# Windowed attention into a squared-ReLU expert layer on one core: the weights' words are joined in a PSUM bank, their low parts go to GpSimd, 15 squares go to VectorE, and the order of work is laid out again

## The chip, the core and the metric

One core of a Trainium2 chip runs the whole program as one launch. The metric is the device time in microseconds; lower is better. The engines are named as the profile names them: PE (TensorE matmul), PEld (its weight loads), DVE (VectorE), ACT (ScalarE), POOL (GpSimd) and SP (SyncE, which issues the DMAs).

## What is computed

The reference, cut to what matters (batch 4, 8 heads, 768 positions, head size 64; 3072 tokens, model width 512, hidden width 2048; all fp32):

```python
for c in range(nc):                     # chunks of 32 queries
    k_full = concat([mem_k, k[:, :, l_start:r_end]])   # 8 memory keys, 16 left, 8 right
    v_full = concat([mem_v, v[:, :, l_start:r_end]])
    a = softmax(scale * q_c @ k_full.T)
    out[:, :, c_start:c_end] = a @ v_full
x = attention output as [3072 tokens, 512]
h = x @ w_in
g = s * maximum(h, 0) ** 2 + b
y = g @ w_out
```

The two weight matrices reach the chip as 64-bit floating point words, seen as pairs of 32-bit integers. The kernel itself turns each into a high fp32r part and a low fp32r part, and every product of the expert layer is made of three matmuls (low x high, high x low, high x high).

## The kernel before, in words

**Tokens and stages.** The tokens fall into five groups: three plain groups of 384 tokens (`ch` 0, 1, 2) and two groups of 960 tokens that are done later by a scheme of seven products on 2x2 blocks (`seven`, `rest`). Attention is done in 40 visits (`attend`): scores on PE, mask and maximum on DVE (`L533`), exponential on ACT (`L537`), a reciprocal and a multiplication by it on POOL (`L546`, `L549`), a transposition on PE (`L558`) or on DVE (`L569`), the product with the values on PE (`L498`).

**Steps.** The plain groups are done in 48 steps (`STEPS`). A step takes one slice `f` of 128 hidden units for one token group: 12 matmuls for h (`hidden`, `L611`), then on ACT relu, square, affine and a high copy in place in a PSUM bank (`L619` to `L622`, the last into `gH`), on DVE the low part `gL` (`L623`), and 9 matmuls into the result (`result`, `L636`). The first 8 steps are group 0 with slices 0 to 7, the next 16 are group 1 with slices 0 to 15, then group 0 with slices 8 to 15, then group 2. So a weight slice that is needed for the first time is met by steps 0 to 7 and 16 to 23. A step is counted from 0; its `gH` is called the first one for step 0.

**Weights.** `weight(i, half, f, due)` turns one of 32 tiles of 128x512 into its two parts. ACT scales the high words into a buffer `wv` (`L586`); DVE shifts the low words (`L587`), joins them with the buffer (`L589`) and puts the sign in (`L591`); ACT copies the result to the high part of `w` (`L595`); DVE subtracts to get the low part (`L596`). One tile thus costs ACT two instructions and DVE four. There are five buffers `wv` and four buffers `words`. Ten tiles come through the `early` buffers. After all tiles are there, `blocks` makes sums of weight blocks for the seven products on POOL (`L694`, `L702`), splits them on ACT and DVE (`L705`, `L706`) and sends them to DRAM.

**The order.** Nothing of the order is written out by hand. Each operation is given an engine, a hold time from the table `HOLD`, a priority (mostly the step at which it is due) and a `lock` flag; `Plan.lay` runs a list scheduler over them at build time, gives out buffers and PSUM banks from rings, and the instructions are then emitted in that order. Operations with the flag on DVE and on POOL are not laid over each other. While a PSUM bank is spare, in the first 40 us of the plan, PE is given filler matmuls (`warm`, `L371`) where it has nothing else. Eight PSUM banks are shared by scores, values, h, result accumulators and products (`room`).

Of the kernel before, what the change touches and what calls it, by code (L numbers as in the profile page):

```python
# [11 lines left out]
F32 = mybir.dt.float32  # L12
F32R = mybir.dt.float32r
I32 = mybir.dt.int32
# [32 lines left out]
LATE_SUMS = 3  # L47
AHEAD = 8.0
# [47 lines left out]
HOP = 2500.0  # L96
WIRE, ALONE = 365.0, 200.0
SLOW, NSLOW, NFIRST = 290.0, 10, 20
FLIGHT = 8
BIG, NEAR = 600, 1500.0  # L100
# [63 lines left out]
class Plan:  # L164
# [25 lines left out]
    def lay(self, filler=None):  # L190
# [18 lines left out]
        while todo:  # L209
# [6 lines left out]
            for e in engines:  # L216
# [37 lines left out]
                if got is None:  # L254
                    if e == "PE" and filler and filler[0](t):
                        laid.append((t, -1, None))
                        free[e] = t + HOLD["warm"]
                        heapq.heappush(events, free[e])
                    continue
# [39 lines left out]
def body(ctx: ExitStack, tc: tile.TileContext, qkv, w1, w2, out):  # L299
# [49 lines left out]
    def room(r, kind):  # L349
        n = r.live.get  # L350
        if kind == "acc":
            r.free += spare
            spare.clear()
            return n("acc", 0) < NT
        if kind == "p":
            return n("p", 0) < 5
# [53 lines left out]
    def anchor(n):  # L410

        ch, c = divmod(n, H // 2)
        if ch == 0:
            return -30 + 2 * c
        if ch < NALONE:
            return starts[ch] - LEAD - 2.0 * (H // 2 - 1 - c)
        i = n - NALONE * (H // 2)
        k = min(i, (NPLAIN - NALONE) * (H // 2) + PB + DEPTH)
        return VISITS[0] + VISITS[1] * k + VISITS[2] * (i - k)
# [156 lines left out]
    def weight(i, half, f, due):  # L576
        src = (w1, w2)[half][f]
        raw = Early(i, 0, 2 * DM) if i < NEARLY - 6 else Val(words)
        v, w = Val(wvs), c_w[half, f]
        both = lambda: raw.tile.bitcast(I32).rearrange("p (n two) -> p n two", two=2)  # L580
        lo, hi = (lambda: both()[:, :, 0]), (lambda: both()[:, :, 1])
        bits = lambda: v.tile.bitcast(I32)
# [3 lines left out]
        op("ACT", "wscale", due, lambda: nc.scalar.activation(v.tile, hi().bitcast(F32), AF.Copy, scale=2.0 ** -112), (raw["hi"],), (v[0],))  # L586
# [3 lines left out]
           (raw["lo"],), (v[0],), lock=True)  # L590
        op("DVE", "wsign", due, lambda: nc.vector.scalar_tensor_tensor(bits(), hi(), -2147483648, bits(), ALU.bitwise_and, ALU.bitwise_or),  # L591
           (raw["hi"],), (v[0],), lock=True)
# [3 lines left out]
        op("DVE", "wjoin", due, lambda: nc.vector.tensor_tensor(  # L596
# [7 lines left out]
    def hidden(u):  # L604
# [13 lines left out]
        ahead = AHEAD if u >= NSLACK else 1.0  # L618
        op("ACT", "relu", u - ahead, lambda: nc.scalar.activation(hp(), hp(), AF.Relu), (), (h[0],))  # L619
        op("ACT", "square", u - ahead, lambda: nc.scalar.activation(hp(), hp(), AF.Square), (), (h[0],))  # L620
# [66 lines left out]
    def blocks(side, g, due):  # L687

        fs = (2 * g, 2 * g + 1)
        parts = [[c_w[side, f]["H"], c_w[side, f]["L"]] for f in fs]  # L690
        sums, high = (Val(words) for _ in range(2))
# [63 lines left out]
    def mix(p):  # L755

        due = base(p) - 6.0
# [230 lines left out]
    for i, (due, half, f) in enumerate(ORDER):  # L988
        weight(i, half, f, due - 1.5)
# [74 lines left out]
```

## Time and profile before, and how to read it

| | us |
|---|---|
| median of 3 runs (595.2 to 597.22) | 595.73 |
| the profiled execution | 596.2 |
| its span, first to last instruction | 594.4 |
| PE busy | 584.0 (98%) |
| PEld busy | 493.7 (83%) |
| DVE busy | 453.1 (76%) |
| ACT busy | 427.2 (72%) |
| POOL busy | 186.2 (31%) |

Busy times are unions over the span; the ends of matmuls are modelled, so a PE that reads 95% busy can still be waiting for operands, and the pace of its matmuls has to be read from their starts. An instruction's own duration is longer than the distance to the next instruction's start on the same engine, since neighbours overlap; costs below are distances between starts where there are rows for them. The averages hide that the engines are loaded differently in different stretches: DVE and ACT are full in the first 100 us and have room later.

### The profile page before, as it was taken

The numbers are of one execution on the slowest core, as the hardware profiler recorded it, in microseconds if no ns is written. First come the engines' busy times: TensorE is split into PE (matmuls) and PEld (weight loads), VectorE is DVE, ScalarE is ACT, GpSimd is POOL, SyncE is SP. The second block draws the span as 40 slices with busy tenths as digits, with TensorE's granted clock in tenths as the row PEclk, the third lists the DMA queues.
The fourth block names the chain that finished last, engine by engine and source line by source line (L and its number), as shares of the span: only waits on it lengthen the run. The fifth ranks groups of instructions, "written<-read, shape, count | busy, mean of one in ns | idle before, by whom it ended". The sixth has DMA issues, their size and how long they took to land.

```text
span 594.4 us, 10771 instructions
## 1 busy us (share of the span) xinstructions
PE 584.0 (98%) x3483; PEld 493.7 (83%) x3487; DVE 453.1 (76%) x1231; ACT 427.2 (72%) x1093; POOL 186.2 (31%) x202
## 2 busy tenths in 40 slices
PE   9999999999999999999999999999999999999997
PEld 4787788888888788888888888888888888888886
DVE  5799999955878877889999777999643443399654
ACT  6999999776878789878787876667533645555552
POOL 4522210187777775713773322000000111000000
PEclk9999999999999999999999999999999999999999
DMA  8953656134899999995789667577766555666761
GB/s 290 406 204 101 224 186 214 63 118 143 277 332 323 358 354 346 320 380 179 259 318 391 244 222 278 194 234 226 241 230 233 207 202 192 207 195 199 241 212 66
DMA packets 71383, 142.78 MB, mean 240 GB/s; under 512 B 7072, under 2 KB 43808, under 8 KB 71328
## 3 DMA queue, kind: packets, MB, share of 16 engines
q1 hardware_dynamic: 71184, 141.99, 70.2%
q8 instruction: 27, 0.44, 0.3%
q14 instruction: 28, 0.23, 0.1%
q10 hardware_dynamic: 144, 0.12, 0.1%
HBM read 102.50 MB, written 39.58 MB: 239 GB/s over the span
## 4 chain that ended last, share of the span: by engine, by line
PE 76%; DVE 10%; ACT 6%; POOL 2%; DMA 2%; issue 2%; SPq 1%; DVEq 0%; POOLq 0%; ACTq 0%
PE ps L824 25%; PE ps L946 25%; PE ps L636 10%; PE ps L611 9%; PE ps L461 4%; PE ps L498 3%; ACT t L537 2%; DVE w L596 2%; DVE t L533 2%; DVE wv L591 2%; DVE wv L589 1%; POOL words L702 1%; ACT wv L586 1%; PE ps L371 1%; DVE words L587 1%
## 5 line engine op out<-in xcount | busy, mean ns | idle before, releaser
L824 PE MATMUL ps<-again,again 128*128 128x480 f32 x672 | 149.0, 381 | 0.0
L824 PEld LDWEIGHTS ps<-again,again 128*128 128x128 f32 x672 | 125.6, 188 | 20.9
L611 PE MATMUL ps<-x,w 128*128 128x384 f32 x576 | 112.3, 340 | 0.3 <-DVE w L596 0.3
L537 ACT ACTIVATE t<-t,nmax 96x128 f32<-96x128 f32 x256 | 99.7, 393 | 13.7 <-DVE nmax L533 13.6
L611 PEld LDWEIGHTS ps<-x,w 128*128 128x128 f32 x576 | 100.4, 188 | 6.6 <-DVE w L596 0.5
L636 PE MATMUL ps<-w,gH 128*128 128x512 f32 x288 | 90.3, 395 | 0.5 <-DVE w L596 0.5
L946 PE MATMUL ps<-gH,again 128*128 128x482 f32 x272 | 81.5, 380 | 0.0
L569 DVE STREAM_TRANSPOSE aT<-t 32x256 f32<-32x256 f32 x168 | 73.0, 435 | 5.4 <-POOL t L549 2.5
L549 POOL TENSOR_TENSOR t<-t,rden 96x1024 f32<-96x1024 f32 (+1 forms) x40 | 61.9, 1552 | 35.1 <-DVE words L587 10.5
L533 DVE CUSTOM_DVE_ANT_0 t<-ps,mask 96x128 f32<-96x128 f32 x256 | 58.5, 281 | 18.2 <-PE ps L461 17.9
L636 PEld LDWEIGHTS ps<-w,gH 128*128 128x128 f32 x288 | 54.0, 188 | 11.2 <-DVE w L596 0.8
L946 PE MATMUL ps<-again,again 128*128 128x482 f32 x264 | 62.0, 382 | 0.0
L636 PE MATMUL ps<-w,gL 128*128 128x512 f32 x144 | 58.2, 404 | 3.8 <-DVE gL L623 3.8
L946 PEld LDWEIGHTS ps<-gH,again 128*128 128x128 f32 x272 | 51.3, 188 | 8.2
L946 PEld LDWEIGHTS ps<-again,again 128*128 128x128 f32 x264 | 49.7, 188 | 8.2
L694 POOL TENSOR_TENSOR words<-w 128x512 f32<-128x512 f32 x32 | 41.3, 1302 | 38.6 <-DVE w L596 20.8
L946 PE MATMUL ps<-gL,again 128*128 128x482 f32 x136 | 51.8, 381 | 0.0
L702 POOL TENSOR_TENSOR words<-words 128x256 f32<-128x256 f32 x64 | 48.2, 754 | 8.0 <-DVE words L706 2.5
L537 ACT ACTIVATION_READ_ACCUMULATOR t<-t,nmax 96x1 f32 x256 | 49.1, 192 | 0.0
L546 POOL TENSOR_SCALAR rden<-den 96x8 f32<-96x8 f32 (+1 forms) x40 | 14.1, 351 | 83.9 <-ACT t L537 81.9
L619 ACT ACTIVATE ps<-ps 128x384 f32<-128x384 f32 x48 | 22.8, 475 | 21.8 <-PE ps L611 21.8
L933 ACT ACTIVATE gH<-again 128x480 fp32r<-128x480 f32 x43 | 25.9, 602 | 17.5 <-PE ps L946 12.5
(103 smaller groups left out, 906.9 us busy)
## 6 DMA issues: line engine op xcount, KB each, us to landing
again<-w1s SPq DMA_DIRECT2D x56, 512.0 KB, 3.7
again<-w2s SPq DMA_DIRECT2D x56, 512.0 KB, 3.8
raw<-qkv SPq DMA_DIRECT2D x28, 448.0 KB, 4.9
words<-w SPq DMA_DIRECT2D x22, 512.0 KB, 4.3
w1s<-words SPq DMA_DIRECT2D x64, 128.0 KB, 3.4
w2s<-words SPq DMA_DIRECT2D x64, 128.0 KB, 4.3
v<-qkv SPq DMA_DIRECT2D x28, 256.0 KB, 4.5
w1s<-w SPq DMA_DIRECT2D x24, 256.0 KB, 4.2
```

Of the source, the lines that this page charges most:

```text
L461: nc.tensor.matmul(scv(n, j), raw.tile[rows, j * (QB + P):j * (QB + P) + QB], raw.tile[rows, j * (QB + P) + QB:(j + 1) * (QB + P)], start= ...
L533: op("DVE", "max", a + 0.1, lambda j=j: nc.vector.tensor_tensor_reduce(t.tile[:, n, j, :], scv(j), mask[:, kinds[j]], -SCALE, 3.0e38, ALU. ...
L537: op("ACT", "exp", a + 0.2, lambda j=j: nc.scalar.activation(t.tile[:, n, j, :], t.tile[:, n, j, :], AF.Exp, bias=nmax()[:, j:j + 1], scal ...
L549: op("POOL", "norm2" if wide else "norm", a + 0.25, lambda: nc.gpsimd.tensor_tensor(t.tile[:, heads], t.tile[:, heads], rden().unsqueeze(3 ...
L569: nc.vector.transpose(aT.tile[gg, :, :, cs], t.tile[cs, :, :, gg])
L611: nc.tensor.matmul(h.tile[:, :TOK], weight_tile(0, f)[:, wi, c * P:(c + 1) * P], x.tile[c][:, xi], start=(c == 0 and n == 0), stop=(c == N ...
L636: nc.tensor.matmul(acc.tile, g.tile[gi][:, t * P:(t + 1) * P], weight_tile(1, f)[:, wi, :], start=(first and n == 0), stop=(last and n == 2))
L694: o = op("POOL", "vsum", due, lambda k=k, f=f: nc.gpsimd.tensor_tensor(at(sums, 2 * k, 2), weight_tile(side, f)[:, 0].bitcast(F32), weight ...
L702: op("POOL", "ssum", due, lambda to=to, a=a, b=b, how=how: nc.gpsimd.tensor_tensor(at(sums, to), at(sums, a), at(sums, b), how), [sums[x] ...
L824: nc.tensor.matmul(bank.tile[:, :PT], w.tile[:, lo:lo + P], xv.tile[xi][:, kc], start=(not more and kc == 0 and i == 0), stop=(kc == 1 and ...
L933: op("ACT", "chigh", due - AHEAD, lambda cut=cut, v=v: nc.scalar.activation(cut.tile[0][:, :PT], at(v), AF.Copy), (part(v),), [cut["H"], * ...
L946: nc.tensor.matmul(sx(bank), w.tile[:, lo:lo + P], cut.tile[xi], start=(first and k == 0), stop=(last and k == 2), skip_group_check=True)
```

## The change

- The scaled high words go into a PSUM bank `b` (kind `"w"`, at most two at once) and are joined there; the sign step reads the bank and writes the buffer `wv`. Join and sign lose their `lock` flag.
- The subtraction for the low part goes to POOL, except for tiles 1, 15, 20 and 27 by the table; one of the entries (25, 28) only repeats the default. Counted in the order of the built program, 28 of the 32 subtractions are on POOL and 4 on DVE.
- In 15 steps (2, 3, 9, 20, 23, 26, 33, 34, 35, 37, 38, 41, 43, 45, 47) ACT writes the relu to a `wv` buffer and DVE multiplies it by max(h, 0) in place, instead of ACT's square.
- A table `NUDGE` moves priorities of visits, weights, steps, block sums and of the last stage's first operands; four constants of the planner's DMA and filler model change, and a filler matmul is not placed where PE has an instruction ready within 450 ns.

The other instructions are the same. In the changed kernel their lines stand 10 to 22 further down. The diff:

```diff
+NUDGE = {
+    ('a', 1): -1.0, ('a', 14): 1.0, ('a', 19): -0.5, ('a', 25): 0.25, ('a', 27): 1.0, ('a', 34): 1.0, ('a', 36): 0.25,
...
+}
-HOP = 2500.0
+HOP = 3000.0
-SLOW, NSLOW, NFIRST = 290.0, 10, 20
+SLOW, NSLOW, NFIRST = 250.0, 10, 20
+COLD, WARMED = 450.0, 5500.0
...
-                    if e == "PE" and filler and filler[0](t):
+                    if e == "PE" and filler and filler[0](t) and not (waiting[e] and waiting[e][0][0] < t + COLD):
                         laid.append((t, -1, None))
-                        free[e] = t + HOLD["warm"]
+                        free[e] = t + (COLD if t < WARMED else HOLD["warm"])
...
+        if kind == "w":
+            return n("w", 0) < 2
...
-        v, w = Val(wvs), c_w[half, f]
+        b, v, w = Val(ps, "w"), Val(wvs), c_w[half, f]
...
-        bits = lambda: v.tile.bitcast(I32)
+        bits = lambda: b.tile.bitcast(I32)
...
-        op("ACT", "wscale", due, lambda: nc.scalar.activation(v.tile, hi().bitcast(F32), AF.Copy, scale=2.0 ** -112), (raw["hi"],), (v[0],))
+        op("ACT", "wscale", due, lambda: nc.scalar.activation(b.tile, hi().bitcast(F32), AF.Copy, scale=2.0 ** -112), (raw["hi"],), (b[0],))
...
-           (raw["lo"],), (v[0],), lock=True)
-        op("DVE", "wsign", due, lambda: nc.vector.scalar_tensor_tensor(bits(), hi(), -2147483648, bits(), ALU.bitwise_and, ALU.bitwise_or),
-           (raw["hi"],), (v[0],), lock=True)
+           (raw["lo"],), (b[0],))
+        op("DVE", "wsign", due, lambda: nc.vector.scalar_tensor_tensor(
+            v.tile.bitcast(I32), hi(), -2147483648, bits(), ALU.bitwise_and, ALU.bitwise_or), (raw["hi"], b[0]), (v[0],))
...
-        op("DVE", "wjoin", due, lambda: nc.vector.tensor_tensor(
+        turn_ = NUDGE.get(("t", i), 1)
+        low, e = ("POOL", nc.gpsimd) if turn_ else ("DVE", nc.vector)
+        op(low, "vsum" if turn_ else "wjoin", due, lambda: e.tensor_tensor(
             dst(1), v.tile, dst(0).bitcast(F32), ALU.subtract), (v[0], w["H"]), (w["L"],), lock=True)
...
-        ahead = AHEAD if u >= NSLACK else 1.0
-        op("ACT", "relu", u - ahead, lambda: nc.scalar.activation(hp(), hp(), AF.Relu), (), (h[0],))
-        op("ACT", "square", u - ahead, lambda: nc.scalar.activation(hp(), hp(), AF.Square), (), (h[0],))
+        ahead = (AHEAD if u >= NSLACK else 1.0) + NUDGE.get(("a", u), 0.0)
+        if NUDGE.get(("q", u), 0):
+            r = Val(wvs, "r")
+            op("ACT", "high", u - ahead, lambda: nc.scalar.activation(r.tile[:, :TOK], hp(), AF.Relu), (h[0],), (r[0],))
+            op("DVE", "low", u - ahead, lambda: nc.vector.scalar_tensor_tensor(hp(), hp(), 0.0, r.tile[:, :TOK], ALU.max, ALU.mult), (r[0],), (h[0],))
+        else:
+            op("ACT", "relu", u - ahead, lambda: nc.scalar.activation(hp(), hp(), AF.Relu), (), (h[0],))
+            op("ACT", "square", u - ahead, lambda: nc.scalar.activation(hp(), hp(), AF.Square), (), (h[0],))
```

The priorities of `anchor` (visits), `blocks`, `mix` and of the call of `weight` get `+ NUDGE.get((kind, number), 0.0)` in the same manner.

How the order moves, at the three places on which the prediction rests. In the changed program's rows `L600` is the scaling, `L601` the shift, `L603` the join, `L605` the sign, `L609` the high part and `L612` the low part of a weight tile (`w`); `L551` is the exponential and `L575` a copy of transposed weights of the attention, `L640`, `L641`, `L642` and `L643` are relu, square, affine and high copy of a step; `L560` and `L563` are the two POOL operations of the attention; `L716` is the first of the block sums.

ACT before, from the sixth `gH` to the seventh:

```order
L622 ACTIVATE gH_172<-ps_179 128x384
L586 ACTIVATE wv_149<-words_150 128x512
L561 ACTIVATE aT_161<-ps_177 128x384
L537 ACTIVATE t_156,den_163<-t_156,nmax_162 96x128 x3
L561 ACTIVATE aT_161<-ps_183 128x384
L595 ACTIVATE w_5_957<-wv_147 128x512
...
L619 ACTIVATE ps_179<-ps_179 128x384
L537 ACTIVATE t_156,den_163<-t_156,nmax_162 96x128
L620 ACTIVATE ps_179<-ps_179 128x384
L595 ACTIVATE w_6_1002<-wv_149 128x512
L621 ACTIVATE ps_179<-ps_179,b_sb,s_sb 128x384
L622 ACTIVATE gH_168<-ps_179 128x384
```

And in the changed program, from the sixth to the seventh:

```order
L643 ACTIVATE gH_172<-ps_178 128x384
L551 ACTIVATE t_157,den_166<-t_157,nmax_165 96x128
L609 ACTIVATE w_7_898<-wv_145 128x512
L600 ACTIVATE ps_183<-words_150 128x512
L600 ACTIVATE ps_180<-words_151 128x512
L640 ACTIVATE ps_179<-ps_179 128x384
L575 ACTIVATE aT_161<-ps_184 128x384
L641 ACTIVATE ps_179<-ps_179 128x384
L642 ACTIVATE ps_179<-ps_179,b_sb,s_sb 128x384
L609 ACTIVATE w_6_935<-wv_146 128x512
L643 ACTIVATE gH_168<-ps_179 128x384
```

Exponentials of the first visits of group 2 stood between the steps and are now behind the sixteenth; ahead of the eighth `gH` there were 74 exponentials and are 64, ahead of the sixteenth 80 and now 69.

DVE before, around the low part of a tile:

```order
L596 TENSOR_TENSOR w_5_857<-wv_149,w_5_857 128x512
L623 TENSOR_TENSOR gL_171<-ps_184,gH_170 128x384
L587 TENSOR_SCALAR words_151<-words_151 128x512
L596 TENSOR_TENSOR w_4_867<-wv_145,w_4_867 128x512
L589 SCALAR_TENSOR_TENSOR wv_146<-wv_146,words_151 128x512
L587 TENSOR_SCALAR words_152<-words_152 128x512
L591 SCALAR_TENSOR_TENSOR wv_146<-words_151,wv_146 128x512
```

And in the changed program, around a moved square (`L638`):

```order
L601 TENSOR_SCALAR words_152<-words_152 128x512
L644 TENSOR_TENSOR gL_173<-ps_180,gH_172 128x384
L638 SCALAR_TENSOR_TENSOR ps_179<-ps_179,wv_147 128x384
L603 SCALAR_TENSOR_TENSOR ps_181<-ps_181,words_152 128x512
L605 SCALAR_TENSOR_TENSOR wv_148<-words_152,ps_181 128x512
L601 TENSOR_SCALAR words_153<-words_153 128x512
L644 TENSOR_TENSOR gL_169<-ps_179,gH_168 128x384
```

Ahead of the eighth `gL` there were 16 low parts on DVE and are 2; ahead of the sixteenth there were 30 and are 4.

POOL before, from the last multiplications of the attention's groups 0 and 1 to the first block sums:

```order
L549 TENSOR_TENSOR t_156<-t_156,rden_164 96x512 x2
L546 TENSOR_SCALAR rden_167<-den_166 96x4 x2
L549 TENSOR_TENSOR t_157<-t_157,rden_167 96x512 x2
L546 TENSOR_SCALAR rden_164<-den_163 96x8
L549 TENSOR_TENSOR t_156<-t_156,rden_164 96x1024
L546 TENSOR_SCALAR rden_167<-den_166 96x8
L694 TENSOR_TENSOR words_152<-w_0_445 128x512
```

And in the changed program, from its twelfth low part and fifteenth multiplication on:

```order
L612 TENSOR_TENSOR w_5_856<-wv_149,w_5_856 128x512
L563 TENSOR_TENSOR t_157<-t_157,rden_167 96x512
L560 TENSOR_SCALAR rden_167<-den_166 96x4
L612 TENSOR_TENSOR w_7_898<-wv_145,w_7_898 128x512
L563 TENSOR_TENSOR t_157<-t_157,rden_167 96x512
L612 TENSOR_TENSOR w_6_935<-wv_146,w_6_935 128x512
...
L612 TENSOR_TENSOR w_15_1333<-wv_149,w_15_1333 128x512
L716 TENSOR_TENSOR words_152<-w_0_455 128x512
```

All 28 low parts on POOL stand ahead of the first block sum. The first 13 of them are mixed with the ninth to the sixteenth multiplication, which belong to group 1.

The filler matmuls are 47 in the order before and 23 in the changed one.

## Rows read from the trace of the kernel before

**Rows 1.** Stretches: length, busy PE, PEld, DVE, ACT, POOL (instructions), clock, DMA share, GB/s.

```profile
0.00:15.00 15.00, 13.80 (x88) 7.15 (x91) 7.59 (x60) 9.10 (x39) 6.99 (x18) 1.00 0.86 291
15.00:30.00 15.00, 14.68 (x160) 10.66 (x159) 12.03 (x64) 15.00 (x63) 8.63 (x13) 1.00 1.03 405
30.00:75.00 45.00, 43.27 (x312) 35.40 (x312) 44.44 (x135) 44.94 (x135) 9.95 (x14) 1.00 0.48 172
75.00:105.00 30.00, 28.51 (x142) 24.96 (x140) 29.94 (x67) 28.17 (x66) 2.49 (x2) 1.00 0.62 211
...
150.00:210.00 60.00, 58.84 (x426) 51.05 (x426) 50.24 (x185) 49.53 (x162) 45.45 (x48) 1.00 1.01 331
```

**Rows 2.** Chain of waits, 105 to 150 us: start, us, what.

```profile
112.45 2.08 PE ps L611 x12
114.53 2.08 PE ps L636 x9
...
147.92 0.81 PE ps L498 x16
```

**Rows 3.** PE in order of time: start, us, line, tiles, count, idle before.

```profile
75.72 2.76 PE L611 MATMUL ps<-x,w 128*128 128x384 f32 x15
...
201.11 0.50 PE L636 MATMUL ps<-w,gL 128*128 128x512 f32 x1 [1.16 <-DVE gL L623]
```

**Rows 4.** Who waited for whom: PE from 75 to 113 us, POOL over the span.

```profile
PE ps L636 <- DVE gL L623: 2.2, 3, 0.8
...
POOL words L694 <- DVE w L596: 20.8, 1, 20.8
```

**Rows 5.** ACT in order of time from 36 us.

```profile
35.66 0.40 ACT L537 ACTIVATE t<-t,nmax 96x128 f32<-96x128 f32 x1
...
36.05 0.48 ACT L619 ACTIVATE ps<-ps 128x384 f32<-128x384 f32 x1
36.46 0.62 ACT L595 ACTIVATE w<-wv 128x512 fp32r<-128x512 f32 x1
36.98 0.48 ACT L620 ACTIVATE ps<-ps 128x384 f32<-128x384 f32 x1
37.38 0.39 ACT L537 ACTIVATE t<-t,nmax 96x128 f32<-96x128 f32 x1
```

**Rows 6.** DVE in order of time, from 36 and from 59 us.

```profile
36.06 0.55 DVE L623 TENSOR_TENSOR gL<-ps,gH 128x384 fp32r<-128x384 f32 x1
36.53 0.42 DVE L587 TENSOR_SCALAR early<-early 128x512 int32<-128x512 int32 x1
...
59.63 0.68 DVE L596 TENSOR_TENSOR w<-wv,w 128x512 fp32r<-128x512 f32 x1
60.23 0.68 DVE L589 SCALAR_TENSOR_TENSOR wv<-wv,words 128x512 int32<-128x512 int32 x1
...
63.13 0.28 DVE L533 CUSTOM_DVE_ANT_0 t<-ps,mask 96x128 f32<-96x128 f32 x1
63.34 0.28 DVE L533 CUSTOM_DVE_ANT_0 t<-ps,mask 96x128 f32<-96x128 f32 x1
```

**Rows 7.** Durations by line: ns minimum/median/maximum, first and last start in us.

```profile
L596 DVE TENSOR_TENSOR w<-wv,w x32: 666/682/1023, 23.4 to 115.9; 128x512 fp32r<-128x512 f32 x32
...
L694 POOL TENSOR_TENSOR words<-w x32: 1272/1302/1327, 116.6 to 304.8; 128x512 f32<-128x512 f32 x32
...
L706 DVE TENSOR_TENSOR words<-words,words x16: 1171/1226/2778, 125.6 to 317.3; 128x1024 fp32r<-128x1024 f32 x16
...
L587 DVE TENSOR_SCALAR words<-words x22: 408/418/422, 54.0 to 110.9; 128x512 int32<-128x512 int32 x22
...
L619 ACT ACTIVATE ps<-ps x48: 463/475/512, 32.7 to 279.8; 128x384 f32<-128x384 f32 x48
...
L622 ACT ACTIVATE gH<-ps x48: 467/490/502, 35.3 to 281.5; 128x384 fp32r<-128x384 f32 x48
...
L623 DVE TENSOR_TENSOR gL<-ps,gH x48: 505/550/558, 36.1 to 282.4; 128x384 fp32r<-128x384 f32 x48
```

More of the change, by code (lines that the diff above doesn't have):

```diff
@@ L412, in anchor @@
         ch, c = divmod(n, H // 2)
+        shift = NUDGE.get(("v", n), 0.0)
         if ch == 0:
@@ L415, in anchor @@
         if ch < NALONE:
-            return starts[ch] - LEAD - 2.0 * (H // 2 - 1 - c)
+            return starts[ch] - LEAD - 2.0 * (H // 2 - 1 - c) + shift
         i = n - NALONE * (H // 2)
         k = min(i, (NPLAIN - NALONE) * (H // 2) + PB + DEPTH)
-        return VISITS[0] + VISITS[1] * k + VISITS[2] * (i - k)
+        return VISITS[0] + VISITS[1] * k + VISITS[2] * (i - k) + shift
     def base(p):
@@ L690, in blocks @@
         parts = [[c_w[side, f]["H"], c_w[side, f]["L"]] for f in fs]
+        due += NUDGE.get(("s", side, g), 0.0)
         sums, high = (Val(words) for _ in range(2))
@@ L755, in mix @@
     def mix(p):
-        due = base(p) - 6.0
+        due = base(p) - 6.0 + NUDGE.get(("m", p), 0.0)
         flat = lambda v: v.tile[:, :2 * PT]
@@ L988, in body @@
     for i, (due, half, f) in enumerate(ORDER):
-        weight(i, half, f, due - 1.5)
+        weight(i, half, f, due - 1.5 + NUDGE.get(("w", i), 0.0))
     for side in range(2):
```

7 rows, old and new, of the table NUDGE are left out of this document.

## The prediction

> **What bounds the kernel now.** I read the stretches first, then the chain of waits, then PE in order of time. In the first 105 us DVE and ACT are the full engines: from 30 to 75 us they are busy for 44.4 and 44.9 of 45 us, from 75 to 105 us for 29.9 and 28.2 of 30, while POOL has 10.0 and 2.5 [rows 1]. PE also reads 95%, but that is modelled ends; its pace tells more. Where PE is free to run, a step costs 2.08 us for its 12 matmuls and 2.08 for its 9 [rows 2], so 4.16. The ninth step (step 8) starts at 75.72 [rows 3], step 16 at 112.45 [rows 2]: 36.7 us for eight steps that cost 33.3, so 3.4 us of waiting, of which 2.2 are matmuls held by the low part gL of DVE [rows 4]. Before 75.72 it is worse: eight steps there. After 112 us the chain lies on PE almost without a break until 148 us [rows 2], and later I found one break, 1.16 us at 201 us, again for gL [rows 3]. So a microsecond that PE gains ahead of 112 us is a microsecond at the end, as long as the others keep up; what DVE, ACT or POOL gain later is worth at most that 1.16 us.
>
> **The change part by part.** I count in the two orders what stands ahead of a point and price it with distances between starts.
>
> *ACT up to the eighth gH.* Exponentials 74, now 64: 10 times 0.39 us (35.66 to 36.05 [rows 5]), 3.9 us less. Two squares are moved to DVE: 2 times 0.40 (36.98 to 37.38 [rows 5]), 0.8 less. One high part more: 0.52 (36.46 to 36.98 [rows 5]). Net 4.2 us less. Up to the sixteenth gH: 11 exponentials and 3 squares fewer, 2 high parts more, 4.3 + 1.2 - 1.0 = 4.5 less. The exponentials are only put off; they are group 2's, which PE meets at step 32, and ACT has room later (49.5 of 60 us from 150 to 210 us [rows 1]).
>
> *DVE up to the eighth gL.* Low parts 16, now 2: 14 times 0.60 (59.63 to 60.23 [rows 6]), 8.4 less. Maxima 74, now 64: 10 times 0.21 (63.13 to 63.34 [rows 6]), 2.1 less. Two squares more at the price of a gL, 0.47 (36.06 to 36.53 [rows 6]), 0.9; one sign more, 0.6. Net 9.0 less. Up to the sixteenth gL it is 26 low parts, 15.6 us, and with the rest about 16.6.
>
> So DVE gets the larger relief and ACT stays the full engine. The nearer limit is ACT, and I take its number: **PE reaches step 8 4.2 us earlier.**
>
> *Steps 8 to 16.* Between the eighth and the sixteenth gH ACT's work hardly changes (4.5 against 4.2). But gL, which held PE for 2.2 of the 3.4 us, comes from an engine with 7.6 us less to do there (16.6 against 9.0). I take half of the 3.4, **1.7 us**; bounds 0 and 3.4.
>
> *The break at 201 us.* Block sums start with the last weight tile, for which POOL waited 20.8 us [rows 4], and that tile comes earlier. Half of 1.16, **0.6 us**; bounds 0 and 1.2.
>
> *The low parts on POOL.* One takes 1.30 there, by the block sums of the same size, against 0.68 [rows 7]. 28 of them are 36.4 us into a stretch in which POOL is busy for 28.1 of 105 us [rows 1], so it fits. What it costs is the way: 0.62 more from a high part to the matmul that needs both. In a chain that runs as a pipeline that enters once, not 28 times. Behind them in POOL's queue stand the multiplications of group 1, of which the eight from the ninth to the sixteenth can each wait for a low part, 1.30 at worst, with the transposition on PE behind. Bounds 0 and 0.6 + 8 x 1.30 = 11.0; I take **1.0 us lost**, near the lower end (the upper end alone would bring the sum to the slow side), because POOL would be busy for only 64 of some 100 us.
>
> A rule speaks against the move: the Trainium skill, GPSIMD Engine Reference, section Engine selection, puts elementwise work on VectorE and calls GpSimd about half as fast for two inputs. The rows agree with its factor (1.30 against 0.68); if it decided, the sum would be 28 x 0.62 = 17 us worse. I don't follow it, because the engine that is left has no time and the other has.
>
> *The detour through PSUM.* No row shows a copy from SBUF into PSUM. An in-place copy in PSUM takes 475 ns, the same from PSUM to SBUF 490 [rows 7]: between 0 and 32 x 0.015 = 0.5 us gained on ACT. Join and sign with one operand in PSUM: gL with such an operand takes 0.55 for 384 columns [rows 6], which scaled in full would be 0.73 for 512 instead of 0.68. So 0 to 64 x 0.05 = 3.2 us more on DVE, 1.8 by the eighth gL. I take nothing for both: what hides it is DVE's distance to ACT, 9.0 - 4.2 = 4.8 us. If collisions on DVE use that up (second rival below), it counts in full. The two banks leave the scores and values fewer; this is in the counted order, where the exponentials went back.
>
> *Squares after step 16, fillers, the rest of the table.* 12 more squares change engines where PE is the bound: nothing. 24 filler matmuls fewer: they fill waits, and the granted clock stays 1.00 with them (2.4 GHz) [rows 1]. Other moves of priority: nothing beyond the counts. SP sends the same transfers; one weight tile is sent ahead of another early.
>
> **The sum.** -4.2 - 1.7 - 0.6 + 1.0 = -5.5 us. The profiled execution took 596.2, its span 594.4, and the median of the runs is 595.73, so 0.5 lower. 590.7 against the profiled one, **590.2** against the median.
>
> **The rivals.**
>
> *First, more.* PE could also gain in the first 30 us: ACT is idle there for 5.9 of the first 15 us [rows 1], with fillers standing ahead of scores on PE. With half of that idle time, the whole 3.4 and the whole 1.16: -4.2 - 3.4 - 1.2 - 3.0 = -11.8, 583.9; the middle between this and the forecast is 587. For it: DVE is relieved by 9 to 17 us. Against: ACT is at 100% from 15 us on [rows 1].
>
> *Second, slower: the two engines get in each other's way.* The split of the block sums on DVE (L706, both inputs in SBUF) took 1.23 us in the median and 2.78 at worst, in a stretch where POOL works most of the time (45.5 of 60 us) [rows 1, 7]: 1.55 us lost in one instruction. The shift (L587) never stretched, 408 to 422 ns [rows 7], but POOL was little used then. If the 18 shifts and 2 low parts ahead of the eighth gL waited for POOL's low parts, DVE's gain of 9.0 would be gone at 0.45 us each. At half of a low part, 0.65 each, it is 13.0 - 9.0 = 4.0 later: 599.7. For it: POOL's share of time goes from a quarter to over a half. Against: join and sign, which were the most time, now have one input from PSUM, as gL has, and gL stays within 505 to 558 ns up to 282 us, through the stretch in which POOL is busiest [rows 7].
>
> The Trainium skill, SBUF — State Buffer, section Who interferes with whom, states this as a rule: a DVE instruction with two SBUF inputs or in a two-port mode, and a GpSimd one, lock each other out for the whole instruction, and one with a single SBUF input isn't concerned. By that rule the shift is still exposed and the join and sign are not; the 2.78 us agrees with it.
>
> *Third, nothing.* ACT is the bound as before, and the exponentials put off come due before PE has used the lead: only the three squares ahead of the sixteenth gH are saved, 1.2 us: 594.5. For it: ACT's work up to the twentieth gH is the same again within 1 us. Against: by then PE has its own queue.
>
> *Fourth, the clock.* With half of the fillers PE might fall to its lower level of 1.2 GHz early; a step would cost 4.16 us more, and at four steps, half of it hidden, the sum would be 2.8 worse than before: 598.5. No row shows any such fall.
>
> **How the numbers follow.** Forecast (4 to 8 us gained) 0.55; first rival 0.17; third 0.16; second 0.09; fourth 0.03. The range of 584.5 to 596.0 takes in the forecast, the third and most of the first, and leaves out the slower ones and a rest of the first. About 0.3% (1.8 us) is what a measurement here can tell from no change. Faster by more: forecast, first, and a third of the third, 0.78. Within: the rest of the third, 0.10. Slower: 0.12.
>
> **What would show it.** Right: the low parts on POOL at 1.3 us; step 8 starts near 71.5, step 16 near 106.5; DVE has idle time from 30 to 105 us and ACT has none to 70; the break at 201 us shrinks. Wrong: shifts of over a microsecond on DVE; PE waiting for `w` from POOL; step 8 no earlier than 75; new breaks of PE between 110 and 300 us because the attention of group 2, now later, isn't ready; a granted clock under 1.00.

## The result, and the profile after

The changed kernel takes **591.17 us** in the median of 4 runs (589.54 to 591.87), the kernel before 596.29 beside it. The ratio is 0.991, with a 95% interval of 0.9886 to 0.9934: 5.1 us faster. The forecast was 590.2 with a range of 584.5 to 596.0. The profiled execution of the changed kernel took 589.54 with a span of 587.8, its fastest run; against the profiled one of before (596.2, span 594.4) it is 6.6 us shorter. Times read from the traces are compared with that 6.6, medians with 5.1.

The stretches of the changed kernel (columns as in [rows 1]):

```profile
0.00:15.00 15.00, 12.02 (x106) 8.13 (x106) 8.61 (x63) 11.45 (x51) 7.85 (x20) 1.00 0.84 286
15.00:30.00 15.00, 14.86 (x137) 10.04 (x134) 13.55 (x63) 14.14 (x52) 8.95 (x13) 1.00 1.03 406
30.00:75.00 45.00, 42.43 (x286) 35.76 (x286) 39.95 (x109) 44.45 (x122) 26.71 (x27) 1.00 0.54 188
75.00:105.00 30.00, 30.00 (x162) 26.64 (x161) 27.54 (x62) 28.30 (x60) 14.16 (x11) 1.00 0.56 191
...
150.00:210.00 60.00, 60.00 (x432) 52.03 (x432) 51.84 (x187) 48.31 (x158) 43.79 (x45) 1.00 1.02 343
```

DVE falls from 44.44 to 39.95 of 45 us between 30 and 75 us and POOL rises from 9.95 to 26.71; ACT stays at 44.45. From 75 us on PE has no gap in the chain, which runs through steps and attention without a wait (chain of waits, 95 to 120 us):

```profile
105.92 2.08 PE ps L627 x12
108.00 1.05 PE ps L475 x16
109.05 2.28 PE ps L657 x9
111.33 2.08 PE ps L627 x12
```

The longest of PE's waits over the whole span. None of all its waits is for `gL` any more, neither the 2.2 us of [rows 4] nor the break at 201 us of [rows 3]; what is left is before 58 us:

```profile
PE ps L627 <- DVE wv L605: 1.5, 1, 1.5
PE ps L475 <- DMA early<-qkv: 1.5, 1, 1.5
PE ps L512 <- ACT aT L575: 0.8, 1, 0.8
...
```

Two rows of PE in order of time. The second holds the last nine matmuls of step 8 (its first three were put ahead, at 67.9), where before it began at 75.72 [rows 3]:

```profile
56.61 2.36 PE L627 MATMUL ps<-x,w 128*128 128x384 f32 x12 [1.54 <-DVE wv L605]
...
71.49 1.72 PE L627 MATMUL ps<-x,w 128*128 128x384 f32 x9
```

Starts of some points in both traces, in us, read off the matmuls of `hidden` and of the low parts `gL`:

| point | before | after | difference |
|---|---|---|---|
| step 0 | 24.7 | 24.5 | -0.2 |
| `gL` of the eighth step | 76.8 | 71.5 | -5.3 |
| step 16 | 112.3 | 105.8 | -6.5 |
| step 17 | 116.4 | 111.2 | -5.2 |
| step 32 | 191.5 | 186.3 | -5.2 |
| step 36 | 215.8 | 209.3 | -6.5 |
| last matmul | 590.2 | 583.6 | -6.6 |

Such a table compares equal amounts of PE work only where the order in between is the same. From step 17 on it is. Between the starts of steps 8 and 17 it isn't: before, PE did 108 matmuls of `hidden` and 81 of `result` there and nothing else, in 40.7 us; after, it does 108, 90, and 32 matmuls for scores and 16 for products with values, in 43.3. The additional work takes 9 x 0.23 + 2 x 1.05 + 0.8 = 5.0 us at PE's free pace. So 5.0 of the 7.8 us by which step 8 begins earlier (75.7 to 67.9) are work that was put behind it, and 2.8 are gained ahead of it; between steps 8 and 17 another 43.3 - 40.7 - 5.0 = -2.4 us are gained. Then nothing changes until the break at 201 us, which brings the last 1.3.

How long the touched instructions take in the changed kernel (columns as in [rows 7]): shift, join, sign, scaling, the low part on POOL, the square on DVE.

```profile
L601 DVE TENSOR_SCALAR words<-words x22: 413/422/1302, 52.0 to 101.3; 128x512 int32<-128x512 int32 x22
L601 DVE TENSOR_SCALAR early<-early x10: 393/418/1201, 17.9 to 49.6; 128x512 int32<-128x512 int32 x10
...
L603 DVE SCALAR_TENSOR_TENSOR ps<-ps,words x22: 677/695/700, 52.7 to 103.7; 128x512 int32<-128x512 int32 x22
...
L605 DVE SCALAR_TENSOR_TENSOR wv<-words,ps x22: 669/683/689, 53.5 to 104.5; 128x512 int32<-128x512 int32 x22
...
L600 ACT ACTIVATE ps<-words x22: 612/634/682, 49.9 to 102.9; 128x512 f32<-128x512 f32 x22
...
L612 POOL TENSOR_TENSOR w<-wv,w x28: 1287/1302/1315, 22.7 to 106.1; 128x512 fp32r<-128x512 f32 x28
...
L638 DVE SCALAR_TENSOR_TENSOR ps<-ps,wv x15: 552/567/567, 39.4 to 273.7; 128x384 f32<-128x384 f32 x15
```

Join and sign have no outlier. The shift has: two of the 32 took 1.20 and 1.30 us, and all that stretched took 2.5 us more than their median together, measured one by one in the trace.

### The profile page after: what moved, and what is told of

Its sections match the earlier page's. It is cut to its first block, busy times and chain, and to the rows that moved or that the text cites. A ratio compares the mean times of both kernels' runs of the same rounds, so it can differ in the third digit from the quotient of the medians.

```text
span 587.8 us, 10784 instructions
## 1 busy us (share of the span) xinstructions
PE 578.3 (98%) x3463; PEld 491.9 (84%) x3463; DVE 444.4 (76%) x1218; ACT 420.6 (72%) x1078; POOL 219.9 (37%) x230
## 4 chain that ended last, share of the span: by engine, by line
PE 91%; DVE 3%; ACT 3%; POOL 1%; DMA 0%; issue 0%; SPq 0%; DVEq 0%; POOLq 0%
PE ps L846 25%; PE ps L968 25%; PE ps L657 16%; PE ps L627 16%; PE ps L475 5%; PE ps L512 4%; ACT t L551 1%; DVE ps L603 1%; DVE wv L605 1%; DVE t L547 1%; ACT ps L600 1%; POOL w L612 0%; PE ps L572 0%; DMA early<-qkv 0%; ACT aT L575 0%
## 5 line engine op out<-in xcount | busy, mean ns | idle before, releaser
L846 PE MATMUL ps<-again,again 128*128 128x480 f32 x672 | 149.0, 381 | 0.0
L846 PEld LDWEIGHTS ps<-again,again 128*128 128x128 f32 x672 | 125.6, 188 | 20.9
L551 ACT ACTIVATE t<-t,nmax 96x128 f32<-96x128 f32 x256 | 99.9, 395 | 22.1 <-DVE nmax L547 21.7
L563 POOL TENSOR_TENSOR t<-t,rden 96x1024 f32<-96x1024 f32 (+1 forms) x40 | 62.1, 1553 | 21.1 <-DVE rden L562 11.8
L551 ACT ACTIVATION_READ_ACCUMULATOR t<-t,nmax 96x1 f32 x256 | 49.5, 193 | 0.0
L612 POOL TENSOR_TENSOR w<-wv,w 128x512 fp32r<-128x512 f32 x28 | 36.3, 1302 | 34.4 <-ACT w L609 21.0
L716 POOL TENSOR_TENSOR words<-w 128x512 f32<-128x512 f32 x32 | 41.3, 1302 | 14.6 <-DMA w1s<-words 4.5
L881 POOL TENSOR_TENSOR againx<-againx 128x480 f32<-128x480 f32 x4 | 4.9, 1237 | 93.5 <-ACT againx L880 93.5
```

Source lines behind the costliest of these rows:

```text
L551: op("ACT", "exp", a + 0.2, lambda j=j: nc.scalar.activation(t.tile[:, n, j, :], t.tile[:, n, j, :], AF.Exp, bias=nmax()[:, j:j + 1], scal ...
L563: op("POOL", "norm2" if wide else "norm", a + 0.25, lambda: nc.gpsimd.tensor_tensor(t.tile[:, heads], t.tile[:, heads], rden().unsqueeze(3 ...
L612: op(low, "vsum" if turn_ else "wjoin", due, lambda: e.tensor_tensor(dst(1), v.tile, dst(0).bitcast(F32), ALU.subtract), (v[0], w["H"]), ( ...
L716: o = op("POOL", "vsum", due, lambda k=k, f=f: nc.gpsimd.tensor_tensor(at(sums, 2 * k, 2), weight_tile(side, f)[:, 0].bitcast(F32), weight ...
L846: nc.tensor.matmul(bank.tile[:, :PT], w.tile[:, lo:lo + P], xv.tile[xi][:, kc], start=(not more and kc == 0 and i == 0), stop=(kc == 1 and ...
```

## The experiments

Two theories. **Relief**: the time comes from DVE and ACT having less to do ahead of step 17, because POOL does the low parts and the exponentials of group 2 stand later; the PSUM bank is what lets POOL and DVE work side by side. **Order**: the time comes from the priorities and from the planner's model; where the subtraction runs matters little. Each run has a ratio to the kernel before on the same chip; a price is that ratio's distance from 0.991, times 596.3 us. The two intervals make such a price uncertain by about 2 us.

**Low parts back on DVE, in the order of the changed kernel.** The order is laid as if they ran on POOL.

```diff
-        low, e = ("POOL", nc.gpsimd) if turn_ else ("DVE", nc.vector)
+        low, e = ("POOL" if turn_ else "DVE"), nc.vector
```

> The changed kernel in its own order, but all 32 low parts are issued on VectorE at the places in the order where GpSimd had 28 of them. Everything else stands where it stood. Theory A (relief of VectorE): VectorE gets 28 x 0.60 = 16.8 us back, 8.4 of it ahead of the eighth gL; it had some 5 us of idle time there and 2.5 from 75 to 105 us, so PE reaches step 16 three to nine us later: 594 to 600 us. Theory B (the order is the gain, the engine doesn't matter): within 1.5 us of the changed kernel, 590 to 592.7.

Measured: 598.66 us (596.88 to 600.12), ratio 1.0035 [1.0018, 1.0053]: 7.5 us lost, more than the whole gain. Its stretch from 30 to 75 us and its waits of PE:

```profile
30.00:75.00 45.00, 39.82 (x251) 32.50 (x249) 41.80 (x121) 40.88 (x113) 7.82 (x12) 0.96 0.42 149
```

```profile
PE ps L657 <- DVE gL L644: 2.5, 5, 1.2
...
PE ps L627 <- DVE wv L605: 2.1, 1, 2.1
```

ACT, whose work is the same, is busy for 40.88 us there instead of 44.45: it now waits for DVE (waits of ACT, 30 to 75 us; the changed kernel has no such row):

```profile
ACT w L609 <- DVE wv L605: 2.9, 6, 0.7
```

No shift stretched in this run. A part of the loss is a thing that I had not counted on: the granted clock falls after PE has idled. Windows from 60 us and the PE row in them:

```profile
60.00:62.00 2.00, 0.43 (x2) 0.43 (x3) 2.00 (x7) 1.82 (x7) 0.00 (x0) 1.00 0.88 345
62.00:64.00 2.00, 2.00 (x10) 2.00 (x9) 2.00 (x6) 1.21 (x4) 0.22 (x1) 0.59 0.72 247
64.00:66.00 2.00, 2.00 (x7) 1.80 (x7) 1.90 (x12) 1.44 (x5) 0.00 (x0) 0.56 0.51 176
66.00:68.00 2.00, 2.00 (x11) 1.70 (x10) 1.67 (x4) 2.00 (x8) 1.04 (x1) 1.00 0.27 104
```

```profile
61.57 3.58 PE L627 MATMUL ps<-x,w 128*128 128x384 f32 x12 [2.14 <-DVE wv L605]
```

The step's 12 matmuls hold PE from 61.57 to 64.95, 3.38 us, where the same step in the changed kernel took 2.20 (56.61 to 58.81); with the three after them it is 1.6 us. So some 5.9 of the 7.5 are DVE's. The times of the run's ten executions agree: the two with a mean clock of 0.999 took 596.9 and 597.6 us, the eight with 0.996 or 0.997 took 597.8 to 600.1. In the trace another 1.6 us are lost by step 0 (26.05 against 24.46), before the first low part runs (24.3).

**All low parts on DVE, laid again for it.** The table's 28 entries for POOL are set to DVE, and the planner knows. The edit, written short:

```diff
+NUDGE.update({("t", i): 0 for i in range(32)})
```

> The changed kernel laid out again with all 32 low parts on VectorE; the join stays in the PSUM bank, the squares stay moved, the shifts of priority stay. Theory A: VectorE has all its work back, 8 to 16 us up to step 16, and the kernel is back at 594 to 599 us. Theory B: 590 to 593 us.

Measured: 599.86 us (599.39 to 601.19), ratio 1.0044 [1.0028, 1.006], 8.0 us lost, a little more than theory A foretold, and no stretch with a lower clock. An order that knows doesn't help: PE waits for `wv` and `gL`, as above.

```profile
PE ps L627 <- DVE wv L605: 3.0, 4, 1.3
PE ps L657 <- DVE gL L644: 2.1, 2, 1.5
```

**About half of them on DVE, in the order of the changed kernel.**

```diff
-        low, e = ("POOL", nc.gpsimd) if turn_ else ("DVE", nc.vector)
+        low, e = ("POOL" if turn_ else "DVE"), (nc.gpsimd if turn_ and i % 2 else nc.vector)
```

> The changed kernel in its own order, 13 of its 28 low parts on POOL (the odd tiles) and 19 on DVE. With none on POOL this order took 598.7, with 28 it takes 591.2. Relief of DVE, each low part taken off it worth the same: 7.5 x 15/28 = 4.0 lost, 595.2. Relief with a threshold (DVE is the limit only once it has more than ACT): most of the gain is there already with 13, 593 or less. All or nothing (a single late tile that sets step 8): 598. Shifts that stretch on DVE: about 3 of 32, in between 0 and 6.

Measured: 593.76 us (591.77 to 594.95), ratio 0.9936 [0.9915, 0.9956]: 1.6 us lost by the ratio, uncertain by 2. All or nothing is out. Between a constant price (4.0 lost, 595.2) and a threshold (593 or less) it doesn't decide. In the trace step 17 starts at 114.1, where it is 111.2 with 28 on POOL and 121.1 with none: 2.9 us for 15 low parts, of which 0.4 were there at step 0 already, and 9.9 for 28, of which 1.6 are the clock and 1.6 were there at step 0. That leaves 0.17 and 0.24 us for each. One shift stretched, 0.8 us.

**Join and sign in SBUF for the first 14 tiles, in the order of the changed kernel.** The scaled words go to an SBUF buffer that is free at that time, instead of the PSUM bank.

```diff
-        bits = lambda: b.tile.bitcast(I32)
+        bk = lambda: outs.tiles[i % 3] if i < 14 else b.tile
+        bits = lambda: bk().bitcast(I32)
...
-        op("ACT", "wscale", due, lambda: nc.scalar.activation(b.tile, hi().bitcast(F32), AF.Copy, scale=2.0 ** -112), (raw["hi"],), (b[0],))
+        op("ACT", "wscale", due, lambda: nc.scalar.activation(bk(), hi().bitcast(F32), AF.Copy, scale=2.0 ** -112), (raw["hi"],), (b[0],))
```

> The changed kernel in its own order, but the first 14 weight tiles are scaled and joined in an SBUF buffer instead of the PSUM bank, so that their join and sign have two SBUF inputs while GpSimd makes low parts. Theory C (both engines share something for SBUF operands): several of the 28 instructions stretch from 0.68 to over 1.0 us, and low parts or multiplications on GpSimd too, the sum some 5 to 12 us on VectorE, the kernel at 593 to 598 us. Rival (only the planner's flag needs the bank): durations stay at 0.68, time within 1 us of 591.2.

Measured: 599.82 us (599.27 to 601.55), ratio 1.0064 [1.004, 1.0088]: 9.2 us lost with the same work on the same engines, more than theory C foretold. Durations of the sign (one line further down in this kernel, `L606`), first the 18 tiles that still use the bank, then those in SBUF, and of the low part (`L613`):

```profile
L606 DVE SCALAR_TENSOR_TENSOR wv<-words,ps x18: 670/684/689, 72.3 to 113.6; 128x512 int32<-128x512 int32 x18
...
L606 DVE SCALAR_TENSOR_TENSOR wv<-early,partial x10: 657/686/1590, 20.8 to 55.0; 128x512 int32<-128x512 int32 x10
L606 DVE SCALAR_TENSOR_TENSOR wv<-words,partial x4: 1560/1576/1666, 57.8 to 67.5; 128x512 int32<-128x512 int32 x4
...
L613 POOL TENSOR_TENSOR w<-wv,w x28: 1285/1300/1934, 22.8 to 115.2; 128x512 fp32r<-128x512 f32 x28
```

With the bank none of 18 exceeds 689 ns; without it four in a row take 1.56 us and more. POOL falls behind too, and PE waits for it:

```profile
PE ps L572 <- POOL t L563: 5.0, 4, 3.5
PE ps L658 <- POOL w L613: 1.8, 2, 0.9
```

The trace is 9.1 us behind the changed kernel at step 7 and no more at step 17. This run has a fall of the granted clock as well (0.96 over 30 to 75 us), so the 9.2 are not the collisions alone.

**Low parts on POOL in the kernel before.** Its order, with join and sign in SBUF for all tiles.

```diff
-        op("DVE", "wjoin", due, lambda: nc.vector.tensor_tensor(
+        e = nc.vector if i in (1, 15, 20, 27) else nc.gpsimd
+        op("DVE", "wjoin", due, lambda: e.tensor_tensor(
```

> The kernel before in its own order, but 28 of its low parts are issued on GpSimd; join and sign stay in SBUF. Theory A alone (relief of VectorE, ScalarE's order unchanged): VectorE loses 16.8 us, ScalarE still has the exponentials ahead: 592 to 595 us. Theory C (two SBUF inputs collide with GpSimd's low parts): join, sign and shift stretch, the relief is given back, 596 to 602 us. Theory B (only the order): within 1 us of the kernel before.

Measured: 606.2 us (604.32 to 610.17), ratio 1.0188 [1.0147, 1.0229]: the move alone makes the kernel before 11 us slower, also more than theory C foretold. Sign (`L591`) and low part (`L597`) stretch, and PE waits for `gL` and for `w`:

```profile
L591 DVE SCALAR_TENSOR_TENSOR wv<-words,wv x22: 637/678/2906, 58.8 to 122.4; 128x512 int32<-128x512 int32 x22
...
L597 POOL TENSOR_TENSOR w<-wv,w x28: 1279/1402/3117, 22.6 to 124.2; 128x512 fp32r<-128x512 f32 x28
```

```profile
PE ps L637 <- DVE gL L624: 5.8, 6, 1.7
PE ps L612 <- POOL w L597: 2.7, 3, 1.8
```

Read one by one, 10 of 32 shifts, 7 joins, 8 signs and 9 low parts exceed their median by over 0.1 us, by 26.6 us in all. The clock is at 1.00 in this stretch, so here it isn't the clock. Both engines stretch: the sign's worst is 2.9 us, the low part's 3.1. How much of the 11 us is the low part's own longer way (1.30 us instead of 0.68, in an order laid for 0.68) wasn't tried apart.

**Squares back on ACT, in the order of the changed kernel.**

```diff
-   op("DVE", "low", u - ahead, lambda: nc.vector.scalar_tensor_tensor(hp(), hp(), 0.0, r.tile[:, :TOK], ALU.max, ALU.mult), (r[0],), (h[0],))
+   op("DVE", "low", u - ahead, lambda: nc.scalar.activation(hp(), r.tile[:, :TOK], AF.Square), (r[0],), (h[0],))
```

> The changed kernel in its own order, but the 15 moved squares run on ScalarE. Theory A (ScalarE is the nearer limit up to step 16, PE after that): three squares ahead of step 16 cost 0.40 us each, the 12 later ones nothing: 591.2 to 592.6 us. Rival (the squares matter all along): 12 more times 0.4, 594 to 597 us.

Measured: 591.14 us (590.45 to 591.9), ratio 0.9914 [0.9892, 0.9935]. The 15 moved squares are worth nothing that can be told from zero: the rival's 594 to 597 is out, the 0 to 1.2 us of theory A is not. In the trace step 8 is 0.2 us later than in the changed kernel and step 16 0.5.

**No shift of priority.** The table keeps its entries on engines (`t` and `q`), the others go, and the order is laid again. The edit, written short:

```diff
+NUDGE = {k: v for k, v in NUDGE.items() if k[0] in "tq"}
```

> The changed kernel laid out again with the table cut to its choices of engine (low parts and squares); all shifts of priority are zero. Ahead of the eighth gH stand 69 exponentials instead of 64, ahead of the sixteenth 80 instead of 69. Theory A (relief by engines, the shifts are small): ScalarE has 2.0 us more ahead of step 8 and 4.3 ahead of step 16, 592 to 595 us. Theory B (the gain is the shifts): 595 to 598 us.

Measured: 595.62 us (594.33 to 596.72), ratio 0.9969 [0.9955, 0.9984]: 3.5 us lost. The median lies in the range of theory B; the ratio, on the 596.3 of the kernel before, gives 594.4, in that of theory A, so the time doesn't decide. PE waits for `gL` again, which the changed kernel never does:

```profile
PE ps L657 <- DVE gL L644: 2.6, 5, 1.6
...
PE ps L846 <- ACT wv L856: 1.0, 1, 1.0
```

By step 17 it is 3.2 us behind the changed kernel (114.4), by the last matmul 5.8 (589.4); the wait at `L846` is at 278 us, where the products begin.

**Only the planner's constants and the filler rule, in the kernel before.**

```diff
-HOP = 2500.0
+HOP = 3000.0
-SLOW, NSLOW, NFIRST = 290.0, 10, 20
+SLOW, NSLOW, NFIRST = 250.0, 10, 20
...
-                    if e == "PE" and filler and filler[0](t):
+                    if e == "PE" and filler and filler[0](t) and not (waiting[e] and waiting[e][0][0] < t + COLD):
...
-                        free[e] = t + HOLD["warm"]
+                        free[e] = t + (COLD if t < WARMED else HOLD["warm"])
```

> The kernel before laid out again with the changed planner constants and the rule on filler matmuls alone. Theory A: VectorE and ScalarE have the same work, within 1.5 us of the kernel before (594.8 to 597.8). Rival (better placed fillers and transfers are the gain): 591 to 594 us.

Measured: 601.05 us (600.45 to 602.11), ratio 1.0063 [1.0042, 1.0084]: 3.8 us slower than before, so both expectations missed. The longest single wait of PE in this trace is for POOL. A multiplication of the attention, 1.04 us a moment before, took 4.44 us while DVE did two shifts, two joins and two signs one after the other, here all in SBUF:

```profile
54.10 1.04 POOL L550 TENSOR_TENSOR t<-t,rden 96x512 f32<-96x512 f32 x1 [1.46 <-DVE wv L592]
...
56.73 4.44 POOL L550 TENSOR_TENSOR t<-t,rden 96x512 f32<-96x512 f32 x1 [1.30 <-DVE w L597]
```

```profile
56.77 0.75 DVE L588 TENSOR_SCALAR words<-words 128x512 int32<-128x512 int32 x2
57.45 1.28 DVE L590 SCALAR_TENSOR_TENSOR wv<-wv,words 128x512 int32<-128x512 int32 x2
58.65 1.28 DVE L592 SCALAR_TENSOR_TENSOR wv<-words,wv 128x512 int32<-128x512 int32 x2
```

```profile
61.22 0.60 PE L559 MATMUL ps<-ident,t 96*128 96x96 f32 x4 [2.87 <-POOL t L550]
```

The fall of the clock follows on this wait (61.6 us in the trace's clock records), so this order met a collision of the kind that the bank takes away. These constants are no gain by themselves; what they are worth in an order without that collision is open.

**Exponentials of group 2 early again.** Two entries bring its first visits forward, and the order is laid again: 73 exponentials ahead of the eighth `gH` instead of 64, 80 ahead of the sixteenth instead of 69.

```diff
+    ('v', 8): -14.0, ('v', 9): -11.0,
```

> The changed kernel laid out again with the first two visits of group 2 given a priority 11 to 14 steps earlier: ahead of the eighth gH stand 73 exponentials instead of 64, ahead of the sixteenth 80 instead of 69. Theory A as it was predicted (ScalarE's work ahead of step 8 is the limit): 9 exponentials of 0.39 us, 3.5 us later at step 8, 593 to 596 us. Rival (they only fill idle time, or what is done early is saved later): within 1 us of 591.2.

Measured: 599.74 us (598.34 to 601.47), ratio 1.004 [1.0022, 1.0059]: 7.8 us lost, about twice what nine exponentials cost on ACT (9 x 0.39 = 3.5). Both expectations missed. Until step 5 the trace is like that of the changed kernel (57.0 against 56.6). Then the rest of the visits comes along: seven transpositions of group 2 stand on DVE ahead of two joins, and PE runs dry for a moment and is granted less (0.96 over 30 to 75 us). DVE and PE in order of time:

```profile
68.65 1.33 DVE L583 STREAM_TRANSPOSE aT<-t 32x256 f32<-32x256 f32 x3
69.99 0.70 DVE L603 SCALAR_TENSOR_TENSOR ps<-ps,words 128x512 int32<-128x512 int32 x1
70.70 1.79 DVE L583 STREAM_TRANSPOSE aT<-t 32x256 f32<-32x256 f32 x4
```

```profile
70.35 3.43 PE L627 MATMUL ps<-x,w 128*128 128x384 f32 x11 [1.09 <-POOL w L612]
```

Since other work moved along, this run doesn't show what ACT's exponentials alone cost.

**All 32 low parts on POOL, laid again with the rest of the table.**

```diff
-    ('t', 1): 0, ('t', 15): 0, ('t', 20): 0, ('t', 25): 1, ('t', 27): 0, ('t', 28): 1,
```

> All 32 low parts on POOL, laid again with the same table. Relief of DVE alone: 4 low parts fewer on DVE, 2.4 us of work, against 4 x 1.30 on POOL; at 0.27 us a low part (7.5 by 28) about 1.1 us faster, 590. POOL as the next limit (w from POOL in PE's waits): 592 to 594. The four exceptions were chosen for an order that fitted them, so that an order laid again loses what its priorities no longer fit: 594 to 596, without a wait on POOL as its main loss.

Measured: 594.82 us (594.46 to 597.09), ratio 0.9963 [0.9947, 0.9979]: 3.2 us lost, though DVE has four low parts less. PE never waits for `w` from POOL; it waits for `gL`:

```profile
PE ps L657 <- DVE gL L644: 2.3, 3, 1.1
```

So POOL is not the next limit. That the loss is that of an order whose priorities no longer fit is what is left of the three expectations; it isn't shown by itself. The traced execution (597.09) is the slowest of the ten.

**No filler matmuls, in the order of the changed kernel.** The 23 fillers are left out when the instructions are written.

```diff
-                warm()
+                pass
```

> The changed kernel in its own order without its 23 filler matmuls; everything else as it is. Clock theory: the granted clock stays at half for longer in the first 40 us, 12 matmuls of a step take more than 2.4 us there, and the sum is some microseconds up, 594 or more. Fillers hide nothing on the way: 591, as before, with the clock at 1.00 in the stretch from 15 to 30 us.

Measured: 593.25 us (592.66 to 593.72), ratio 0.9933 [0.9908, 0.9957]: 1.4 us lost by the ratio, which the intervals don't separate from nothing. The trace shows more: step 0 starts at 27.8 instead of 24.5, and 3.1 of the 3.3 us stay to the last matmul (586.7 against 583.6). With the fillers, five traces in this order have step 0 between 24.3 and 26.1, so 2 to 3.5 us are the fillers'. The same groups of four transpositions, without the fillers:

```profile
20.03 0.90 PE L572 MATMUL ps<-ident,t 96*128 96x96 f32 x4
...
21.66 0.55 PE L572 MATMUL ps<-ident,t 96*128 96x96 f32 x4
```

and with them, in the changed kernel:

```profile
8.71 0.49 PE L572 MATMUL ps<-ident,t 96*128 96x96 f32 x4
10.86 0.55 PE L572 MATMUL ps<-ident,t 96*128 96x96 f32 x4
```

Without fillers they take 0.90 us up to 20 us and 0.55 from 21.66 on; with them 0.49 to 0.55 from 8.71 on. Both expectations erred: the sum stayed below 594, and yet the slow matmuls are there.

## Why the prediction was right

**Relief was shown, and the bank and the order are its conditions.** Taking the low parts back costs 7.5 us in the same order and 8.0 in one laid for it, more than was gained. But the same move without the bank costs the kernel before 11 us, and without the shifts of priority 3.5 of the gain is lost. The pieces don't add up to 5.1: three of them are each worth most of it, since each is needed. Without the shifts the change still gains 1.8 us on the kernel before (ratio 0.9969); with the shifts, but with all low parts on DVE, it loses 2.6 (1.0044).

**ACT up to step 8, -4.2, and POOL's way, +1.0: together -3.2.** Measured ahead of step 8, with the moved work taken out: -2.8. That nine of step 8's matmuls stand at 71.49, where 71.5 was foretold, is chance: its first matmul is at 67.88, and 5.0 us of other work were put behind it. That ACT has hardly any idle time from 30 to 70 us and DVE has was right.

The reason is only in part borne out. I took the smaller of two reliefs, ACT's, as the one that counts. No run shows this: the one run that gives ACT more to do in the same order, that of the squares (which DVE then has less), made step 8 0.2 us later in the trace, where 2 x 0.40 = 0.8 would be due. What can be tested is DVE's side, of which I treated the 4.8 us beyond ACT's relief as cover. By that, giving 14 low parts (8.4 us) back to DVE ahead of the eighth `gL` costs 8.4 - 4.8 = 3.6 us. In the trace step 8 is then 6.5 us later; without the 1.6 of the clock and the 1.6 that were there at step 0, 3.3. So far the reckoning holds. By the sixteenth `gL` it gives 15.6 - (16.6 - 4.5) = 3.5 in all, and the trace has lost 9.9 - 1.6 - 1.6 = 6.7 at step 17. There two sums side by side are not enough. The engines are links of one round as well: ACT scales, DVE joins and signs, ACT copies, and ACT's 2.9 us of waiting for `wv` in that run show that one holds up the other.

**Steps 8 to 16, -1.7** (bounds 0 and 3.4). Measured up to step 17: -2.4, and PE's waits for `gL` are gone, as the step said. Half of the 3.4 was too cautious. A reader who takes step 16 alone finds -6.5, near the announced 106.5 (105.8), but a part of that is one group of scores that had not been done yet.

**The break at 201 us, -0.6** (bounds 0 and 1.2). Measured: it is gone. From step 32 to 36, with the same matmuls in both, 24.3 became 23.0 us, -1.3. The first block sum starts at 107.5 us instead of 116.6, as foretold; that this is what removed the break was not tried.

**POOL, +1.0** (bounds 0 and 11.0). The low part takes 1.302 us, as foretold from the block sums, and no wait of PE for `w` is in the list. The +1.0 itself can't be read apart from the first term. That the GpSimd is half as fast for this, which the Trainium skill gives in GPSIMD Engine Reference, section Engine selection, as the reason to stay on VectorE, is true here (1302 against 684 ns) and still the wrong choice: in this kernel VectorE has no time and GpSimd has.

**The bank, nothing** (0 to -0.5 on ACT, 0 to +3.2 on DVE). In the 22 tiles that come through `words` the medians of join and sign are 17 and 5 ns above those of before (678 both), some 0.5 us for all 32. The scaling is 634 ns instead of 670, in the ten early tiles 650 instead of 662, so 0.9 us for 32 tiles, beyond my bound, since I had judged by a copy from PSUM into SBUF. Both are small. What I had not weighed is what the bank is for; I named that only as the word against the second rival.

**Squares, nothing:** the time agrees (591.14), with an uncertainty of 2 us. **Other moves of priority, nothing:** not settled. I wrote "nothing beyond the counts", and the run without the shifts lost 3.5 us; but it also has 5 more exponentials ahead of the eighth `gH` and 11 more ahead of the sixteenth, for which my prices give 2.0 and 4.3 us. So the counts may be all of it, and I can't tell from that run where the order's worth comes from. **Fillers, nothing:** the 23 that are left are worth 2 to 3.5 us at step 0 in the traces; what the 24 fewer cost was not tried apart.

Sum by the traces: -2.8 - 2.4 - 1.3 = -6.5 against the forecast -5.5, and 5.1 by the medians.

**The rivals.** *More* would have needed the first 15 us; step 0 gained 0.2. *Slower, in each other's way*: two shifts of over a microsecond, a sign that I had announced as one against me, did come, but 2.5 us in all, 1.8 of them ahead of the eighth `gL`, instead of the 9.0 that it takes. The mechanism is real, and the two runs without the bank show it at full size; the planner's constants show it on POOL's side. The Trainium skill, SBUF — State Buffer, section Who interferes with whom, says that a DVE instruction with two SBUF inputs and a GpSimd one lock each other out and that one with a single SBUF input doesn't; the runs agree for join and sign (none of 64 stretched with the bank, 15 of 64 in the kernel before with low parts on POOL), and the shift, which that page leaves exposed if it runs in a two-port mode, stretched in 6 of 32. *Nothing* is out by the interval. *The clock*: no fall in the changed kernel. "No row shows any such fall" held for the trace of before; four of the slower variants show one.

None of the runs was faster than the changed kernel beyond its uncertainty.

## What to carry to other kernels

Work taken off a full engine is worth what that engine holds up, not its own duration: here 0.60 us of DVE work for each low part became 0.2 us at the end (5.9 by 28), and a slow idle engine was the right place for it. Before work goes to GpSimd, look at which DVE instructions in that stretch read two operands from SBUF, and give one of them a PSUM operand first. When a planner lays the order, compare the amounts of work between two points before a difference of starts is called a gain.

## What the runs showed of the hardware that I had not expected

- **The granted clock can fall in the middle of a kernel.** In four runs (low parts on DVE in the order of the changed kernel, join in SBUF, the planner's constants, exponentials early) it falls once between 60 and 75 us, after PE had idled; in the first of them the trace's clock records give 0.50 (1.2 GHz instead of 2.4) from 62.3 to 65.8 us, of which the windows shown have 0.59 and 0.56, and PE loses 1.6 us by it. A lost microsecond of feeding thus cost more than itself.
- **The clock column can hide a slow start.** In the run without fillers it reads 1.00 in each of the first stretches, while four transpositions take 0.90 us instead of 0.55. Time for which the trace has no clock record counts as 1.00 there: this run's first record, of 1.00, begins at 21.3 us, between the last slow group (20.03) and the first fast one (21.66). In the changed kernel it begins at 6.9 us and in the kernel before at 8.1, so the 1.00 from 0 to 15 us in [rows 1], on which the prediction's word on the fillers rests, has a slow start in it too. In the five traces with fillers in the changed kernel's order it begins between 6.9 and 11.1 us. The Trainium skill, TensorE: Matmul & The Clock Gate, section Seeing it yourself, warns not to trust the records of the gate alone; here records and durations agree, and it is the column's mean that misleads.
- **A collision can double an instruction in a row:** four signs of 1.56 to 1.67 us against 0.68, with two SBUF inputs beside a busy POOL. It can be worse on POOL's side: 4.44 us for a multiplication of 1.04, beside joins and signs one after the other.
